# Filler matmuls through the first half of the first chunk's first MoE, in a fused attention and MoE kernel

## Chip, core, metric

One NeuronCore of a Trainium2 chip. The metric is the device time of one execution in microseconds (us), the median of several runs. Before the change it is 1012.5 us (three runs, 1010.94 to 1013.31).

## What is computed

A linear attention with decay over 4 batches, 8 heads, 768 steps and head size 48; its output, as 3072 tokens of 384 numbers, goes through two mixture-of-experts style feed-forward layers (here called the first and the second MoE; each has one expert).

```
for t in range(S):
    cur = einsum('bhd,bhe->bhde', u * k[t], v[t])
    y[t] = einsum('bhd,bhde->bhe', r[t], state + cur)
    state = w[t] * state + einsum('bhd,bhe->bhde', k[t], v[t])
x = y as [B*S, 384]
xn = x / sqrt(mean(x*x) + 1e-6) * rms_g
x = (silu(xn @ w_gate) * (xn @ w_val)) @ w_out        # 384 -> 1536 -> 384
h = relu(x @ w_in)
out = (s * h * h + b) @ moe2_w_out                    # 384 -> 2048 -> 384
```

## The kernel before

The 768 steps are cut into 6 chunks of 128. For each chunk and each of the 4 batches (24 pairs, numbered `jb`) `attention` builds decay products on VectorE (the scans of L340 and L347), scores on TensorE (L379), transposes of k (L383), a small product with u (L388), the masked scores on VectorE (`a`, by L303), the sums `y` (L429, and L422 with the state from chunk 1 on), the new state (L442) and the current step's part (L446). `y` is then normalised on ScalarE and GpSimd, turned by TensorE (L517, in `attention_x`) and split into a high and a low half, `xh` and `xl` (L525), for products in float32r of near float32 accuracy.

A MoE step takes 128 columns of the hidden width (`f`). `mm_in` (L590) makes nine matmuls per product, three pairs of halves times three slices of the 384 inputs; ScalarE and VectorE make the hidden values `sg`, split into `hh` and `hl`; `mm_out` (L575 to L577 in `mm3`) adds three output slices into PSUM banks 2, 3 and 4 over all `f`. The weights come as 64-bit words and are turned into float32 halves, by VectorE for the most part (`weights`, L554 to L566), in the time of the first chunks. The first MoE's first six `f` (`FA`) run over chunk 0 and then chunk 1, then the other six over both; in the first of these four parts the first four `f` go in halves of 256 columns (two batches), the other two over 512.

No engine's order is written out. Every step is given to `Plan.add` with a due time, a cost per engine and the buffers that it reads and writes. `Plan.issue` (L129) is a list scheduler: it walks through time, gives each engine that is free the earliest due step whose inputs are there, and writes the steps out in that order. Each engine's queue runs in that order on the chip, whatever the real times are.

PSUM has 8 banks, `PS`. The attention of chunk 0 takes its banks in turn from a ring (`bank`, L314), six per `jb`: two for scores, one for k's transpose, one for `y`, one for the new state, one for the turned `x`.

A filler is one matmul of zeros, 128x512 in bfloat16, with a weight load of zeros (`idle`, L774). The program begins with 14 of them (`warm`), and the planner adds one wherever it finds PE free with nothing ready, and books `FILL` us for it (L153 to L156). It stops doing so at the first step in `plan.ends`, the first `mm_in`.

Of the kernel before, what the change touches and what calls it, by code (L numbers as in the profile page):

```python
# [22 lines left out]
B, H, S, D = 4, 8, 768, 48  # L23
# [4 lines left out]
KD = DM // 128  # L28
# [20 lines left out]
FA, HALF = 6, (4, 6)  # L49
# [51 lines left out]
class Plan:  # L101
# [6 lines left out]

    PASS = {"pe": 0.20, "pool": 0.10, "act": 0.15, "dve": 0.12, "sp": 2.0}
    SHARED = 6.0  # L110
    FILL = 0.22

    def __init__(self):
        self.idle, self.ends = (None, None), set()
        self.ops, self.deps, self.wrote, self.read = [], [], {}, {}

    def add(self, when, engines, fn, reads=(), writes=(), port=True):
# [82 lines left out]
def mm(n, k=1):  # L200
    return k * (0.013 + n / 2400.0)
# [3 lines left out]
def body(ctx: ExitStack, tc: tile.TileContext, rkw, nat, w1, w2, cst, out):  # L205
    nc = tc.nc
    sb = ctx.enter_context(tc.tile_pool(name="sb", bufs=1))
    ps = ctx.enter_context(tc.tile_pool(name="ps", bufs=1, space=PSUM))
# [67 lines left out]
    plan = Plan()  # L276
# [12 lines left out]
    def op(when, engines, fn, reads=(), writes=(), port=True):  # L289
        if planned[0]:  # L290
            reads, writes = [alias.get(k, k) for k in reads], [alias.get(k, k) for k in writes]
            plan.add(when, engines, fn, reads, writes, port)
        else:
            fn(next(iter(engines)))
# [15 lines left out]
    def ring(name, of):  # L310
        rings[name] = rings.get(name, -1) + 1
        return of[rings[name] % len(of)]

    def bank(jb):  # L314
        return ring("q", (5, 6, 7, 2, 3, 4)) if jb < B else ring("at", (5, 6, 7))

    BOTH = ("dve", "pool")
    DVE, POOL = ("dve",), ("pool",)
# [251 lines left out]
    def slots_of(ph, f):  # L570
        return range(3 * f, 3 * f + 3) if ph == 0 else range(2 * f, 2 * f + 2)
# [7 lines left out]
    def mm_in(t, i, s, x, b0=0, nb=B):  # L579
        n, sl = nb * C, slice(b0 * C, (b0 + nb) * C)  # L580

        dst = PS[i][:, 0:n]

        parts = [[(k, x, b, kk) for b in range(b0, b0 + nb) for kk in range(KD)] for k in ("xh", "xl")]
        passes = ((0, XH), (1, XH)), ((0, XL),)

        def run(e, some, first, last):
            for kk in range(KD):
                for j, (w, xx) in enumerate(some):
                    nc.tensor.matmul(  # L590
                        dst, W[s][:, w, kk * 128:(kk + 1) * 128], xx[x][:, kk, sl], start=first and j == kk == 0,
                        stop=last and kk == KD - 1 and j == len(some) - 1, skip_group_check=True)

        if planned[0] and not plan.ends:
            plan.ends.add(len(plan.ops))
        if t < T0 + 2.0 and planned[0]:
            for p in range(2):
                op(t, {"pe": mm(n, 6 - 3 * p)}, lambda e, p=p: run(e, passes[p], p == 0, p == 1),
                   [("wh", s), ("wl", s)] + parts[p], [("ps", i)])
        else:  # L600
            op(t, {"pe": mm(n, 9)}, lambda e: run(e, ((0, XH), (0, XL), (1, XH)), True, True),
               [("wh", s), ("wl", s)] + parts[0] + parts[1], [("ps", i)])

    def mm_out(t, banks, s, q, first, last, b0=0, nb=B, h0=0):
        n, sl = nb * C, slice(b0 * C, (b0 + nb) * C)
        hs = slice(h0 * C, (h0 + nb) * C)
        for m in range(KD):
            op(t, {"pe": mm(n, 3)}, lambda e, m=m: mm3(
                PS[banks[m]][:, sl], W[s], slice(m * 128, (m + 1) * 128), HH[q][:, hs], HL[q][:, hs],
                first, last), [("wh", s), ("wl", s), ("hh", q), ("hl", q)], [("ps", banks[m])])  # L610

    def store(t, banks, dst, key, b0=0, nb=B):
        n, sl = nb * C, slice(b0 * C, (b0 + nb) * C)
# [132 lines left out]
    def start():  # L746
# [24 lines left out]
                nc.gpsimd.memset(g.rearrange("p h j d -> p (h j d)"), 0.0)  # L771

        def idle():
            nc.tensor.matmul(PS[0], zero[:, 0:128], zero, start=True, stop=True)  # L774

        def warm(e):
            for _ in range(NWARM):
# [5 lines left out]
        op(-199, {"pool": 1.6}, empty, (), [("st", b, p) for b in range(B) for p in range(2)], False)  # L783
        op(-299, {"act": 2.8}, lambda e: nc.scalar.activation(tab, half, AF.Silu), ["c"], ["tab"])
        plan.idle = idle, len(plan.ops)
        op(-300, {"pe": 5.0}, warm, ["z"], [("ps", 0)])

    start()
    steps = []
# [197 lines left out]
```

## Time and profile before

| | us |
|---|---|
| Median of three runs | 1012.5 |
| The profiled execution | 1013.5 |
| Span of its instructions | 1011.6 |
| TensorE busy | 993.0 |
| VectorE busy | 668.9 |
| ScalarE busy | 404.0 |
| GpSimd busy | 215.7 |

PE is TensorE, PEld its weight loads, DVE is VectorE, ACT ScalarE, POOL GpSimd, SP the engine that issues the DMAs. A matmul's row is longer than its share of PE's time, since the next one starts before it ends; what one costs is the distance from its start to the next. The granted clock (PEclk) is a share of 2.4 GHz: 1.00, or 0.50, which is 1.2 GHz. Times in the views are from the span's start.

### The profile page before, as it was taken

To read this page: it belongs to the slowest core of one execution; us is meant where nothing else is said; L and a number is where in the kernel's file an instruction comes from. 1 tells how busy PE (TensorE), PEld (TensorE's weight loads), DVE (VectorE), ACT (ScalarE), POOL (GpSimd) and SP (SyncE) were. 2 spreads that over 40 slices of the span, in tenths; PEclk is the share of its full clock that TensorE was granted. 3 is DMA by queue.
4 is the path that set the end of the run, shared out by engine and by line. 5 is a ranking of instruction groups with operands and counts; after the bars stand their busy time and mean duration, and the time that the engine had idled before them with its cause. 6 is when DMAs were issued, how large, how long until landed. Compare 5 with 4: busy or idle time off the path is not lost.

```text
span 1011.6 us, 14993 instructions
## 1 busy us (share of the span) xinstructions
PE 993.0 (98%) x5873; PEld 834.0 (82%) x5873; DVE 668.9 (66%) x1106; ACT 404.0 (40%) x791; POOL 215.7 (21%) x258
## 2 busy tenths in 40 slices
PE   8989999999999999999999999999999999999997
PEld 5879899888888888888888888887888888888885
DVE  8789997365665565555579889999994443433432
ACT  3334553243554454444434335343343433433333
POOL 4203310114455444445223432000000000000000
PEclk9679999999999999999999999999999999999999
DMA  7343662122221131122276556766660000000001
GB/s 244 111 143 107 212 192 74 40 71 83 83 62 52 51 92 50 52 88 63 68 209 188 177 167 203 250 201 228 235 228 1 1 32 1 32 1 0 32 1 35
DMA packets 44991, 105.19 MB, mean 104 GB/s; under 512 B 3953, under 2 KB 19569, under 8 KB 44913
## 3 DMA queue, kind: packets, MB, share of 16 engines
q1 hardware_dynamic: 44912, 104.16, 32.7%
q8 instruction: 48, 0.79, 0.3%
q14 instruction: 31, 0.25, 0.1%
HBM read 93.14 MB, written 11.01 MB: 103 GB/s over the span
## 4 chain that ended last, share of the span: by engine, by line
PE 95%; DVE 1%; issue 1%; DMA 1%; ACT 1%; POOL 0%; DVEq 0%; ACTq 0%; POOLq 0%
PE b L590 48%; PE b L575 11%; PE b L576 11%; PE b L577 11%; PE b L379 3%; PE b L429 2%; PE b L422 2%; PE b L434 1%; PE b L442 1%; PE b L383 1%; PE b L517 1%; PE b L388 1%; PE b L774 1%; DMA out_t<-o 1%; PE b L446 1%
## 5 line engine op out<-in xcount | busy, mean ns | idle before, releaser
L590 PE MATMUL b<-xh,w 128*128 128x512 f32 (+1 forms) x1566 | 489.4, 377 | 0.5 <-ACT sg L306 0.5
L590 PEld LDWEIGHTS b<-xh,w 128*128 128x128 f32 x1566 | 290.8, 191 | 52.4 <-ACT sg L306 0.7
L590 PE MATMUL b<-xl,w 128*128 128x512 f32 (+1 forms) x783 | 293.0, 375 | 0.0
L575 PE MATMUL b<-hh,w 128*128 128x512 f32 (+1 forms) x537 | 206.6, 385 | 1.8 <-ACT hh L306 1.1
L576 PE MATMUL b<-hl,w 128*128 128x512 f32 (+1 forms) x537 | 203.4, 379 | 2.3 <-DVE hl L303 2.0
L577 PE MATMUL b<-hh,w 128*128 128x512 f32 (+1 forms) x537 | 202.4, 377 | 0.0
L306 ACT ACTIVATE sg<-b 128x512 f32<-128x512 f32 (+1 forms) x179 | 102.1, 571 | 230.9 <-PE b L590 229.4
L590 PEld LDWEIGHTS b<-xl,w 128*128 128x128 f32 x783 | 149.3, 191 | 25.1
L659 DVE SCALAR_TENSOR_TENSOR sg<-sg,cs,b 128x512 f32<-128x512 f32 (+1 forms) x97 | 71.8, 741 | 99.0 <-ACT sg L306 98.9
L576 PEld LDWEIGHTS b<-hl,w 128*128 128x128 f32 x537 | 101.5, 189 | 22.0 <-DVE hl L303 2.4
L575 PEld LDWEIGHTS b<-hh,w 128*128 128x128 f32 x537 | 101.4, 189 | 21.0 <-ACT hh L306 1.7
L577 PEld LDWEIGHTS b<-hh,w 128*128 128x128 f32 x537 | 101.4, 189 | 18.3
L662 DVE SCALAR_TENSOR_TENSOR hl<-sg,cs,hh 128x512 fp32r<-128x512 f32 (+1 forms) x97 | 73.0, 753 | 50.2 <-ACT hh L306 50.2
L306 ACT ACTIVATE hh<-sg,cs 128x512 fp32r<-128x512 f32 (+1 forms) x97 | 69.7, 719 | 84.2 <-DVE sg L659 78.9
L306 ACT ACTIVATE hh<-sg 128x512 fp32r<-128x512 f32 (+1 forms) x82 | 47.5, 579 | 112.7 <-DVE sg L303 112.6
L303 DVE TENSOR_TENSOR sg<-b,sg 128x512 f32<-128x512 f32 (+1 forms) x82 | 51.1, 623 | 51.3 <-PE b L590 49.8
L303 DVE TENSOR_TENSOR hl<-sg,hh 128x512 fp32r<-128x512 f32 (+1 forms) x82 | 53.7, 654 | 13.7 <-ACT hh L306 13.3
L566 POOL TENSOR_TENSOR w<-pat,w 128x384 fp32r<-128x384 f32 x28 | 36.1, 1306 | 65.5 <-ACT w L564 65.5
L401 POOL TENSOR_SCALAR_AFFINE_SELECT a<-a 128x512 f32<-128x512 f32 x38 | 33.1, 890 | 64.7 <-ACT a L306 64.7
L564 ACT ACTIVATE w<-pat 128x384 fp32r<-128x384 f32 x68 | 32.9, 519 | 30.3 <-DVE pat L560 28.7
L560 DVE SCALAR_TENSOR_TENSOR pat<-raw,pat 128x768 uint32<-128x768 uint32 (+1 forms) x40 | 36.1, 908 | 0.0
L558 DVE SCALAR_TENSOR_TENSOR pat<-raw,pat 128x768 uint32<-128x768 uint32 (+1 forms) x40 | 35.8, 899 | 0.1
(122 smaller groups left out, 1011.9 us busy)
## 6 DMA issues: line engine op xcount, KB each, us to landing
raw<-in_w SPq DMA_DIRECT2D x56, 768.0 KB, 4.4
in<-in_rkw SPq DMA_DIRECT2D x24, 448.0 KB, 4.0
raw<-in_w SPq DMA_DIRECT2D x24, 384.0 KB, 3.5
n<-in_nat SPq DMA_DIRECT2D x16, 384.0 KB, 3.1
in<-in_rkw SPq DMA_DIRECT2D x24, 226.6 KB, 2.6
x2d<-o SPq DMA_DIRECT2D x21, 256.0 KB, 2.6
a<-in_rkw SPq DMA_DIRECT2D x24, 224.0 KB, 3.7
v<-in_nat SPq DMA_DIRECT2D x24, 192.0 KB, 3.1
```

The source lines that it names most:

```text
L303: op(when, {e: cost[e] for e in engines}, lambda e: E[e].tensor_tensor(dst, a, b, f), reads, writes, port)
L306: op(when, {"act": act(n)}, lambda e: nc.scalar.activation(dst, src, func, **kw), reads, writes)
L401: op(t, {"pool": 0.60}, lambda e, s=A[p]: nc.gpsimd.affine_select(out=AT[s], in_=AT[s], compare_op=ALU.is_gt, fill=0.0, base=0, pattern=[[ ...
L558: op(t, {"dve": vec2(N)}, lambda e, word=word, pat=pat: nc.vector.scalar_tensor_tensor(pat(), word(1), 0xC0000000, pat(), ALU.bitwise_and, ...
L560: op(t, {"dve": vec2(N)}, lambda e, word=word, pat=pat: nc.vector.scalar_tensor_tensor(pat(), word(0), 29, pat(), ALU.logical_shift_right, ...
L566: op(t, {"dve": vec2(DM)} if ph == 0 else {"dve": vec2(DM), "pool": gps(DM)}, lambda e, c=c, s=s, pat=pat: E[e].tensor_tensor(W[s][:, 1], ...
L575: nc.tensor.matmul(dst, wt[:, 0, cols], xh, start=first, stop=False, skip_group_check=True)
L576: nc.tensor.matmul(dst, wt[:, 0, cols], xl, start=False, stop=False, skip_group_check=True)
L577: nc.tensor.matmul(dst, wt[:, 1, cols], xh, start=False, stop=last, skip_group_check=True)
L590: nc.tensor.matmul(dst, W[s][:, w, kk * 128:(kk + 1) * 128], xx[x][:, kk, sl], start=first and j == kk == 0, stop=last and kk == KD - 1 an ...
L659: op(t, {"dve": vec2(n)}, lambda e: nc.vector.scalar_tensor_tensor(sg, sg, s_col, p, ALU.mult, ALU.mult), [("ps", i)], [("sg", q)], False)
L662: op(t, {"dve": vec2(n)}, lambda e: nc.vector.scalar_tensor_tensor(hl, sg, b_col, hh.bitcast(F32), ALU.add, ALU.subtract), [("sg", q), ("h ...
```

## The change

Four edits. The planner goes on with fillers until the first output step of the sixth `f` of the first part (its weight slot is `slots_of(0, FA - 1)[2]`). It books 0.17 us for each in place of 0.22. The fillers write bank 4, not bank 0: until the first output step has written bank 4 they start afresh (`start=True`), after it they add their zeros to what stands there (`plan.opened`). Bank 4 leaves the ring of chunk 0's attention, which has five banks left.

```diff
--- before.py
+++ after.py
@@ -108,10 +108,10 @@
 
     PASS = {"pe": 0.20, "pool": 0.10, "act": 0.15, "dve": 0.12, "sp": 2.0}
     SHARED = 6.0
-    FILL = 0.22
+    FILL = 0.17
 
     def __init__(self):
-        self.idle, self.ends = (None, None), set()
+        self.idle, self.ends, self.opened = (None, None), set(), False
         self.ops, self.deps, self.wrote, self.read = [], [], {}, {}
 
     def add(self, when, engines, fn, reads=(), writes=(), port=True):
@@ -312,7 +312,7 @@
         return of[rings[name] % len(of)]
 
     def bank(jb):
-        return ring("q", (5, 6, 7, 2, 3, 4)) if jb < B else ring("at", (5, 6, 7))
+        return ring("q", (5, 6, 7, 2, 3)) if jb < B else ring("at", (5, 6, 7))
 
     BOTH = ("dve", "pool")
     DVE, POOL = ("dve",), ("pool",)
@@ -591,8 +591,6 @@
                         dst, W[s][:, w, kk * 128:(kk + 1) * 128], xx[x][:, kk, sl], start=first and j == kk == 0,
                         stop=last and kk == KD - 1 and j == len(some) - 1, skip_group_check=True)
 
-        if planned[0] and not plan.ends:
-            plan.ends.add(len(plan.ops))
         if t < T0 + 2.0 and planned[0]:
             for p in range(2):
                 op(t, {"pe": mm(n, 6 - 3 * p)}, lambda e, p=p: run(e, passes[p], p == 0, p == 1),
@@ -604,10 +602,15 @@
     def mm_out(t, banks, s, q, first, last, b0=0, nb=B, h0=0):
         n, sl = nb * C, slice(b0 * C, (b0 + nb) * C)
         hs = slice(h0 * C, (h0 + nb) * C)
+        if planned[0] and s == slots_of(0, FA - 1)[2]:
+            plan.ends.update(range(len(plan.ops), len(plan.ops) + KD))
+
+        def run(e, m):
+            plan.opened = plan.opened or banks[m] == 4
+            mm3(PS[banks[m]][:, sl], W[s], slice(m * 128, (m + 1) * 128), HH[q][:, hs], HL[q][:, hs], first, last)
+
         for m in range(KD):
-            op(t, {"pe": mm(n, 3)}, lambda e, m=m: mm3(
-                PS[banks[m]][:, sl], W[s], slice(m * 128, (m + 1) * 128), HH[q][:, hs], HL[q][:, hs],
-                first, last), [("wh", s), ("wl", s), ("hh", q), ("hl", q)], [("ps", banks[m])])
+            op(t, {"pe": mm(n, 3)}, lambda e, m=m: run(e, m), [("wh", s), ("wl", s), ("hh", q), ("hl", q)], [("ps", banks[m])])
 
     def store(t, banks, dst, key, b0=0, nb=B):
         n, sl = nb * C, slice(b0 * C, (b0 + nb) * C)
@@ -771,7 +774,7 @@
                 nc.gpsimd.memset(g.rearrange("p h j d -> p (h j d)"), 0.0)
 
         def idle():
-            nc.tensor.matmul(PS[0], zero[:, 0:128], zero, start=True, stop=True)
+            nc.tensor.matmul(PS[4], zero[:, 0:128], zero, start=not plan.opened, stop=True, skip_group_check=True)
 
         def warm(e):
             for _ in range(NWARM):
@@ -783,7 +786,7 @@
         op(-199, {"pool": 1.6}, empty, (), [("st", b, p) for b in range(B) for p in range(2)], False)
         op(-299, {"act": 2.8}, lambda e: nc.scalar.activation(tab, half, AF.Silu), ["c"], ["tab"])
         plan.idle = idle, len(plan.ops)
-        op(-300, {"pe": 5.0}, warm, ["z"], [("ps", 0)])
+        op(-300, {"pe": 5.0}, warm, ["z"], [("ps", 4)])
 
     start()
     steps = []
```

PE's order has 132 fillers after the change and had 47; all its other steps are the same steps. Two products of the state with the decay (L303, 48x192) go from GpSimd's order to VectorE's. The last 4,958 rows of PE's order are the same in both. Two places of it follow. In the names `b_152` to `b_159` are the PSUM banks 0 to 7, `sv_111` the zeros, `in_124` and `in_125` the inputs of the even and the odd `jb`, `xg_135` normalised rows of `y`, `w_75` and up the weight slots.

The first place is PE behind the first batch's attention (`jb` 0), where the second's begins. Before (of the eight L379 rows two stand here):

```order
L446 MATMUL b_154<-av_136,cs_63 128x384
L379 MATMUL b_157<-in_125 128x128
L379 MATMUL b_158<-in_125 128x128
L383 MATMUL b_159<-cs_63,in_125 128x112 x4
L774 LDWEIGHTS sv_111
L774 MATMUL b_152<-sv_111 128x512
L388 MATMUL b_159<-cs_63,l_107 128x2 x4
```

After (one of 22 fillers in a row, and one of two, stand here):

```order
L446 MATMUL b_154<-av_136,cs_63 128x384
L777 LDWEIGHTS sv_111
L777 MATMUL b_156<-sv_111 128x512
L517 MATMUL b_157<-cs_63,xg_135 128x128 x3
L379 MATMUL b_158<-in_125 128x128
L379 MATMUL b_159<-in_125 128x128
L383 MATMUL b_154<-cs_63,in_125 128x112 x4
L388 MATMUL b_154<-cs_63,l_107 128x2 x4
```

The second batch's scores (L379) stood right behind the first batch's last step; now 22 fillers and the turn of the first batch's rows (L517) are between, and its k's transpose goes to bank 2, where the first batch's `y` was.

The second place is PE from the turn of the second batch's rows to the first MoE step's end. After (each row that only repeats is left out):

```order
L517 MATMUL b_158<-cs_63,l_109 128x128 x3
L379 MATMUL b_159<-in_124 128x128
L383 MATMUL b_155<-cs_63,in_124 128x112 x4
L590 MATMUL b_152<-xh_112,w_75 128x256 x6
L388 MATMUL b_155<-cs_63,n_128 128x2 x4
L429 MATMUL b_157<-v_126,a_132 128x48 x4
L442 MATMUL b_158<-v_126,kt_131 64x48
L446 MATMUL b_157<-av_136,cs_63 128x384
L590 MATMUL b_152<-xl_114,w_75 128x256 x3
L590 MATMUL b_153<-xh_112,w_76 128x256
L777 LDWEIGHTS sv_111
L777 MATMUL b_156<-sv_111 128x512
```

Before, five fillers stood behind that L517, then the two products of L590, then the third batch's attention, and no filler came after. Now 19 fillers stand ahead of L517, none from there to the end of the two products, and 15 behind them. Further groups follow: 8 and 6 around the fourth batch's L517, 11 and 15 around the third `f`'s output steps, 2 and 4 in the fifth `jb`.

## Rows read from the trace of the kernel before

**Rows 1.** The page's part 1: busy us, share of the span, instructions

```profile
PE 993.0 (98%) x5873; PEld 834.0 (82%) x5873; DVE 668.9 (66%) x1106; ACT 404.0 (40%) x791; POOL 215.7 (21%) x258
```

**Rows 2.** Waits of PE, 145 to 1012 us: total, times, longest

```profile
PE b L575 <- ACT hh L306: 1.1, 1, 1.1
PE b L575 <- ACT in L623: 0.7, 1, 0.7
PE b L576 <- DVE hl L662: 0.3, 1, 0.3
```

**Rows 3.** The page's part 2: granted clock in 40 slices of 25.3 us

```profile
PEclk9679999999999999999999999999999999999999
```

**Rows 4.** Stretches of 2 us: length, busy by engine, then granted clock, DMA share, GB/s

```profile
32.00:34.00 2.00, 1.58 (x19) 1.49 (x19) 2.00 (x5) 0.78 (x3) 0.00 (x0) 0.60 0.79 229
...
58.00:60.00 2.00, 2.00 (x12) 2.00 (x12) 1.78 (x6) 0.59 (x2) 0.00 (x0) 0.57 0.01 4
...
66.00:68.00 2.00, 2.00 (x14) 2.00 (x13) 2.00 (x4) 0.91 (x2) 0.00 (x0) 0.63 1.02 349
68.00:70.00 2.00, 2.00 (x12) 2.00 (x12) 1.16 (x3) 0.00 (x0) 0.00 (x0) 0.51 0.73 259
```

**Rows 5.** Fillers: weight loads of L774 (ns min/median/max, starts), then PE's timeline, start and us

```profile
L774 PEld LDWEIGHTS <-sv x47: 95/98/181, 1.3 to 26.5; 128*128 128x128 bf16 x47
...
22.09 3.62 PE L774 MATMUL b<-sv 128*128 128x512 bf16 x16
25.54 0.49 PE L517 MATMUL b<-cs,l 128*128 128x128 f32 x3
```

**Rows 6.** PE's timeline, 30 to 66 us; in brackets the idle time ahead and its releaser

```profile
32.42 1.09 PE L442 MATMUL b<-v,kt 128*64 128x48 f32 x16 [0.63 <-ACT kt L306]
...
43.48 1.09 PE L442 MATMUL b<-v,l 128*64 128x48 f32 x16 [0.63 <-ACT l L306]
...
56.36 0.90 PE L517 MATMUL b<-cs,l 128*128 128x128 f32 x3 [2.24 <-ACT l L306]
...
61.58 0.28 PE L576 MATMUL b<-hl,w 128*128 128x256 f32 x1
61.70 0.28 PE L577 MATMUL b<-hh,w 128*128 128x256 f32 x1
...
65.04 0.38 PE L576 MATMUL b<-hl,w 128*128 128x256 f32 x1 [1.97 <-DVE hl L303]
```

**Rows 7.** PE's timeline, 8 to 16 us: the first batch, and the second's scores

```profile
8.56 1.16 PE L379 MATMUL b<-in 48*128 48x128 f32 x16 [1.79 <-DVE in L303]
9.65 0.60 PE L383 MATMUL b<-cs,in 112*128 112x112 f32 x4
...
10.31 0.95 PE L388 MATMUL b<-cs,n 112*128 112x2 f32 x8
...
11.77 1.88 PE L429 MATMUL b<-v,a 128*128 128x48 f32 x16
13.58 0.67 PE L442 MATMUL b<-v,kt 128*64 128x48 f32 x16
14.17 0.91 PE L446 MATMUL b<-av,cs 128*128 128x384 f32 x2
15.01 1.16 PE L379 MATMUL b<-in 48*128 48x128 f32 x16
```

**Rows 8.** Waits of DVE, 34 to 70 us: the three largest

```profile
DVE w L566 <- ACT w L564: 3.2, 1, 3.2
DVE a L303 <- PE b L379: 3.2, 1, 3.2
DVE av L303 <- ACT l L306: 2.2, 1, 2.2
```

**Rows 9.** Waits of PE, 70 to 145 us

```profile
PE b L383 <- DVE xl L525: 0.8, 1, 0.8
PE b L590 <- ACT sg L306: 0.5, 1, 0.5
```

## The prediction, made before the change was run

> **What bounds the kernel now.** I read five views, from coarse to fine. The first, the page's busy line, has TensorE (PE) busy for 993.0 of 1011.6 us and VectorE (DVE), the next, for 668.9 [rows 1]. The reader should see that PE leads, but not yet that it decides, since matmuls overlap. The second is the waits of PE from 145 us to the end: three, 2.1 us in sum [rows 2]. From 145 us on PE simply works through its list, so whatever brings it to that point later or earlier moves the end by as much. The third, the page's 40 slices, says where the first 145 us lose time: PE's granted clock is 6 and 7 tenths in the second and third slice and at the top after that [rows 3]. The fourth, stretches of 2 us, dates it. 0.60 between 32 and 34 us is a full clock (2.4 GHz) until 32.4 us and half (1.2 GHz) from there; 0.57 puts the return at 59.72; 0.63 and 0.51 give a second low stretch from 66.52 to 69.96 [rows 4]. That is 27.32 + 3.44 = 30.76 us at half speed. The fifth, PE's timeline, gives what PE did before the clock fell: after the last filler at 26.5 us [rows 5] came 2.5 us of L590 and then the third batch's attention, many short matmuls and a wait of 0.63 us [rows 6]. The attention of the first two batches, with fillers between its parts, lies before the fall.
>
> The four waits of PE between 30 and 70 us are 0.63 (ACT's copy of kt), 0.63 (the same, next batch), 2.24 (L517 on the normalised rows) and 1.97 us (L576 on `hl`): 5.47 us [rows 6]. The second and third, 2.87 us, lie in the low stretch, so PE worked 30.76 - 2.87 = 27.9 us at half speed. At the full clock that work takes half, so the low clock costs 13.9 us.
>
> **The change, part by part.** PE's time up to 145 us is useful work at the full clock, plus the extra of a low clock, plus waits, plus fillers. The useful work is the same before and after (the order differs in 85 fillers and otherwise in sequence), and the last 4,958 of PE's rows are the same. So the sum needs three terms.
>
> *Fillers.* 132 in place of 47. One costs the distance from start to start: 16 of them from 22.09 to 25.54 us, 0.2156 us each [rows 5]. 85 x 0.2156 = 18.3 us added. Their weight loads lie beside them (98 ns each). They wait for nothing after the first, because the zeros are ready at the start and bank 4 is written by PE alone until the part's end. Now some of them accumulate where all before overwrote; no row of before shows that for these matmuls, but L576 and L577, which both accumulate into one bank, start 0.12 us apart, about what 256 columns need [rows 6], so I take no surcharge.
>
> *The planner's 0.17.* It books 0.17 us for what takes 0.2156. A planned gap thus gets more fillers than fit it, and PE comes 0.046 us later per filler to the step behind. That is inside the 18.3 us. It has a good side: a group outlasts the wait that it covers. The wait for L517 was 3.45 us in the second batch (22.09 to 25.54 us, [rows 5]); the new groups in front of L517 have 22, 19, 15 and 8+ fillers, that is 4.7, 4.1, 3.2 and 1.7 us.
>
> *Five banks in place of six.* The second batch's scores now stand behind the first batch's L517 and 22 fillers: in place of 15.01 us [rows 7] they start at about 15.0 + 22 x 0.2156 + 0.3 = 20.1 us, 5 us later. Since the time is filled with fillers it is not counted again. What is late next is VectorE: its mask and the `xl` of each batch move back, so the third batch's mask comes some 2 us later than now. The bounds of a new PE wait from this: nothing, if the fillers overrun it; 3.2 us, the largest wait of VectorE on this chain now, at the top [rows 8]. Two state products move from GpSimd to VectorE, beside PE.
>
> *What the clock gives back.* If the clock holds at 2.4 GHz through the first part, 13.9 us, and with the fillers in place of waits up to 5.47 us more: 19.4 us.
>
> Sum: 19.4 - 18.3 = 1.1 us gained, less new waits between 0 and 3.2 us. I take 0.5, near the lower end, because I followed the new order by hand with the full-clock durations of [rows 7] and found L517, the masks and the split weights ready before PE got through its fillers nearly every time. That leaves **-0.6 us**. It is a wash: the fillers take the time that the clock returns. The profiled execution took 1013.5 us, its span 1011.6; the three timed runs have a median of 1012.5, so the profiled one is 1.0 above. By its own time the change gives 1012.9; against the median 1012.5 - 0.6 = **1011.9 us**. A measurement of this kernel tells about 0.2%, 2.0 us, from no change.
>
> **Rivals.**
>
> *The clock falls all the same, in the third batch* (slower). In the new order PE runs from the second batch's L517 to the next 15 fillers without one: scores, transposes, six L590, L388, L429, L442, L446 and the rest of the first two L590 groups. From the rows of the first batch that is 1.1 + 0.6 + 0.7 + 0.9 + 1.8 + 0.6 + 0.8 + 1.4 = 7.9 us (18 L590 at 0.12; L383 and L388 by their own durations, the others from start to start) [rows 6, 7]. Before, the clock fell 5.9 us after the last filler, with much the same work [rows 4, 5]. For it: the same mix and no filler. Against it: no wait stands in the stretch now, and the first batch's 11.8 to 15.0 us, with no filler either, kept the full clock. It decides if the granted clock drops between about 33 and 40 us. The price of one low stretch is half of 3.44 us; two of them, 3.4 us: 1015.3 us. Chance 0.15. The Trainium skill bears on this (TensorE: Matmul & The Clock Gate, "A second HAM failure mode: psum-queue depth-cycling"): a kernel that cycles through PSUM banks makes PE pause briefly between groups so often that its clock swings between two levels. The trace agrees that a fall needs no long wait; by that rule five banks in place of six speak against this change, and the time would be this rival's.
>
> *The waits after 70 us go too* (faster). Two waits remain in before, 0.8 us at L383 and 0.5 us at L590 [rows 9]. If VectorE is ahead there by then, and no new wait comes, 19.4 + 1.3 - 18.3 = 2.4 us: 1010.1 us. VectorE's three largest waits between 34 and 70 us, 3.2, 3.2 and 2.2, are the room for it [rows 8]. Chance 0.15.
>
> *The weights come late* (slower). The chain of five banks puts the first four batches in series, and VectorE, which splits the weights too, then leaves PE waiting behind the fillers. The point from which it decides is a delay of VectorE that outlasts the groups; with the upper bound of 3.2 us and no 0.5, 1011.9 + 2.7 = 1014.6 us. Chance 0.07.
>
> *PE is not the bound* (much faster). If the fillers lay in time that PE has to spare, the 18.3 us would cost nothing and the whole 19.4 us stay: 993.1 us. Against it: 2.1 us of waits in 866 us [rows 2]. Chance 0.02. The Trainium skill (Perfetto Trace Analysis, "Identifying the Most-Contended Engine") says that matmul busy time is a poor measure of what TensorE has left and the busy share of the weight loads a better one. That share is 82% here [rows 1], which by the rule leaves room; I go by the waits, which leave none.
>
> *The change does not do what it says.* Fillers of zeros might not hold the clock among attention steps; then the low stretches stay, the fillers come on top, and with the waits they replace it is 1012.5 + 18.3 - 5.5 = 1025.3 us. Against it: before, with fillers, the clock was full until 32.4 us. Chance 0.03.
>
> **How the numbers follow.** The forecast, a clock that holds and a small remainder, has 0.58. Its own range is 1010.8 (no new wait, and part of the waits after 70 us) to 1014.4 (near the upper bound of the waits): all within 0.2% but for its edges. Faster by over 0.2%: 0.15 + 0.02 = 0.17. Slower: 0.15 + 0.07 + 0.03 = 0.25. Same: 0.58. The range takes in the faster rival at 1010.1 and the slower at 1015.3 and leaves out 993 and 1025, 1 in 20, and the tails of the rest: 1009.9 to 1015.4.
>
> **What the profile after would show.** Right: granted clock at the top from the first slice to the last but the start; 132 fillers of about 28 us in sum counted start to start; PE waits between 10 and 145 us under 2 us; VectorE's three largest waits between 34 and 70 us under 5 us in sum. The first rival: a stretch of 2 us with a clock of 0.5 to 0.8 between 33 and 45 us. The weights' rival: new PE waits on `w` or `hl` behind a group of fillers. I am wrong in the main if PE's fillers and useful work after 70 us no longer add up to the span, or if PE shows waits after 145 us that are not there now.

## The result and the profile after

The changed kernel is **slower by 0.7%**: 1016.78 us, the median of 18 runs (1012.62 to 1022.27), against 1010.66 for the kernel before, run beside it on the same chips (18 runs, 1003.57 to 1019.24). The ratio is 1.0071, with a 95% interval of 1.0050 to 1.0093. The forecast was 1011.9, at most 1015.4. The profiled execution took 1018.22 us. Runs over 1.5% above the fastest of the same kernel count as slow and are left out of the ratios and of what is fitted below: one of these 18 (1019.24), and 13 of the 130 of the kernel before that were made beside the experiments (1021 to 1026 us, at mean clocks of 0.973 to 0.979).

The page of the kernel after: its span, the busy line, the granted clock, and the fillers' group.

```profile
span 1016.5 us, 15168 instructions
...
PE 1005.5 (99%) x5958; PEld 834.7 (82%) x5958; DVE 667.1 (66%) x1108; ACT 403.9 (40%) x791; POOL 210.3 (21%) x256
...
PEclk7999999999999999999999999999999999999999
...
L777 PE MATMUL b<-sv 128*128 128x512 bf16 x132 | 35.7, 421 | 1.3 <-DVE col L759 1.3
```

Read it against [rows 1, 3]. PE is busier by 12.5 us; GpSimd is less busy by 5.4 us, and the other engines do what they did. The two low slices in the time of the MoE, 6 and 7 tenths in [rows 3], are full now. A low one has appeared where none was, in the first slice. The stretches of 2 us date it (same columns as [rows 4]):

```profile
8.00:10.00 2.00, 0.90 (x12) 0.90 (x14) 2.00 (x3) 0.00 (x0) 0.00 (x0) 0.91 1.06 381
10.00:12.00 2.00, 2.00 (x14) 1.46 (x11) 2.00 (x5) 0.00 (x0) 0.59 (x2) 0.50 0.99 363
...
22.00:24.00 2.00, 2.00 (x8) 0.75 (x6) 0.06 (x1) 0.53 (x2) 1.64 (x5) 0.68 0.88 295
24.00:26.00 2.00, 2.00 (x11) 0.88 (x9) 0.00 (x0) 0.59 (x2) 0.00 (x0) 1.00 0.19 77
...
66.00:68.00 2.00, 2.00 (x13) 1.13 (x13) 2.00 (x5) 0.20 (x1) 0.00 (x0) 1.00 0.66 201
68.00:70.00 2.00, 2.00 (x15) 1.58 (x14) 2.00 (x5) 0.00 (x0) 0.00 (x0) 1.00 0.33 97
```

0.91 of a full clock between 8 and 10 us is a fall to half (1.2 GHz) at 9.64; 0.68 is the return (2.4 GHz) at 23.28. From there on every stretch is at 1.00, those around 66 to 70 us too, which were low before [rows 4]. The low time is 13.6 us, not 30.8, and lies under the first batch's attention instead of the third's. What PE did before the fall: it ran its first fillers, waited 1.77 us for VectorE's `in`, and began the first scores.

PE's waits from 0 to 145 us, all of 0.2 us and more, then (after the "...") from 145 us to the end:

```profile
PE b L379 <- DVE in L303: 1.8, 1, 1.8
PE b L777 <- DVE col L759: 1.3, 1, 1.3
...
PE b L575 <- ACT in L626: 0.7, 1, 0.7
PE b L575 <- DVE o L628: 0.2, 1, 0.2
```

Both of the first two stood there before too (the 1.79 in [rows 7] is one). The four waits of [rows 6] and the two of [rows 9] are gone, 6.8 us, and 1.2 of the 2.1 us after 145 us [rows 2].

PE's timeline where the second batch begins:

```profile
20.98 6.06 PE L777 MATMUL b<-sv 128*128 128x512 bf16 x22
26.88 0.49 PE L517 MATMUL b<-cs,xg 128*128 128x128 f32 x3
27.30 1.16 PE L379 MATMUL b<-in 48*128 48x128 f32 x16
```

The second batch's scores start at 27.30 us; before it was 15.01 [rows 7], and the prediction said 20.1. The low clock made the first batch 6 us late, and the fillers are the other 6.

The sum of these two executions, each row of PE taken from its start to the next one's, less idle time: fillers take 32.8 us in place of 12.1 (85 x 0.2156 is 18.3; most of the rest is that 11 of them ran at the half clock), useful rows 972.6 in place of 980.9, and PE idles 4.5 us in place of 11.9. That is +20.7 - 8.2 - 7.4 = +5.1 us to PE's last row; the spans differ by 4.9.

The useful rows ran 9.3 us at the half clock in place of 27.9, and gave back 8.2, less than half of the difference: in these traces a row does not take quite twice as long at the half clock. Two rows of the kernel before, in its second low stretch, start 0.21 us apart; the same two lines at the full clock start 0.12 apart [rows 6]:

```profile
67.24 0.41 PE L576 MATMUL b<-hl,w 128*128 128x256 f32 x1
67.45 0.41 PE L577 MATMUL b<-hh,w 128*128 128x256 f32 x1
```

### The profile page after: what moved, and what is told of

It reads as the page before. It is cut to its first block, busy times and chain, and to the rows that moved or that the text cites. A ratio compares the mean times of both kernels' runs of the same rounds, so it can differ in the third digit from the quotient of the medians.

```text
span 1016.5 us, 15168 instructions
## 1 busy us (share of the span) xinstructions
PE 1005.5 (99%) x5958; PEld 834.7 (82%) x5958; DVE 667.1 (66%) x1108; ACT 403.9 (40%) x791; POOL 210.3 (21%) x256
## 4 chain that ended last, share of the span: by engine, by line
PE 91%; DVE 4%; DMA 3%; issue 1%; ACT 1%; POOL 0%; SPq 0%; ACTq 0%; DVEq 0%
PE b L590 45%; PE b L575 10%; PE b L576 10%; PE b L577 10%; PE b L379 3%; PE b L777 2%; PE b L429 2%; PE b L422 2%; PE b L434 1%; PE b L442 1%; PE b L383 1%; PE b L517 1%; DVE ws L720 1%; PE b L388 1%; DMA xl<-x2d 1%
## 5 line engine op out<-in xcount | busy, mean ns | idle before, releaser
L590 PE MATMUL b<-xh,w 128*128 128x512 f32 (+1 forms) x1566 | 486.8, 375 | 0.1
L590 PEld LDWEIGHTS b<-xh,w 128*128 128x128 f32 x1566 | 287.6, 188 | 52.6 <-DVE sg L303 0.3
L590 PE MATMUL b<-xl,w 128*128 128x512 f32 (+1 forms) x783 | 291.5, 373 | 0.0
L576 PE MATMUL b<-hl,w 128*128 128x512 f32 (+1 forms) x537 | 202.9, 378 | 0.4
L590 PEld LDWEIGHTS b<-xl,w 128*128 128x128 f32 x783 | 147.4, 188 | 25.6
L576 PEld LDWEIGHTS b<-hl,w 128*128 128x128 f32 x537 | 101.1, 188 | 20.5 <-DVE hl L665 2.5
L577 PEld LDWEIGHTS b<-hh,w 128*128 128x128 f32 x537 | 101.0, 188 | 18.3
L303 DVE TENSOR_TENSOR sg<-b,sg 128x512 f32<-128x512 f32 (+1 forms) x82 | 51.1, 624 | 58.0 <-PE b L590 54.8
L303 DVE TENSOR_TENSOR hl<-sg,hh 128x512 fp32r<-128x512 f32 (+1 forms) x82 | 53.6, 654 | 15.2 <-ACT hh L306 15.0
L566 POOL TENSOR_TENSOR w<-pat,w 128x384 fp32r<-128x384 f32 x28 | 33.7, 1219 | 68.2 <-ACT w L564 68.2
L401 POOL TENSOR_SCALAR_AFFINE_SELECT a<-a 128x512 f32<-128x512 f32 x38 | 28.9, 781 | 71.5 <-ACT a L306 71.5
L525 DVE SCALAR_TENSOR_TENSOR xl<-b,cs,xh 128x128 fp32r<-128x128 f32 x72 | 20.8, 345 | 28.8 <-ACT xh L306 28.7
L777 PE MATMUL b<-sv 128*128 128x512 bf16 x132 | 35.7, 421 | 1.3 <-DVE col L759 1.3
```

Source lines behind the costliest of these rows:

```text
L303: op(when, {e: cost[e] for e in engines}, lambda e: E[e].tensor_tensor(dst, a, b, f), reads, writes, port)
L566: op(t, {"dve": vec2(DM)} if ph == 0 else {"dve": vec2(DM), "pool": gps(DM)}, lambda e, c=c, s=s, pat=pat: E[e].tensor_tensor(W[s][:, 1], ...
L576: nc.tensor.matmul(dst, wt[:, 0, cols], xl, start=False, stop=False, skip_group_check=True)
L577: nc.tensor.matmul(dst, wt[:, 1, cols], xh, start=False, stop=last, skip_group_check=True)
L590: nc.tensor.matmul(dst, W[s][:, w, kk * 128:(kk + 1) * 128], xx[x][:, kk, sl], start=first and j == kk == 0, stop=last and kk == KD - 1 an ...
L777: nc.tensor.matmul(PS[4], zero[:, 0:128], zero, start=not plan.opened, stop=True, skip_group_check=True)
```

## Experiments

My first theory was that the change is mostly a trade of fillers against the clock, in which the fillers cost more than they return. The rivals put the loss on one of the three other edits: five banks in place of six, the planner's 0.17, or where the fillers lie. Every run also carries its mean granted clock, which turned out to be the most useful number: for most kernels here the time follows it nearly in a straight line (not for e9_pow, whose clock hardly moved, and e14_half). Below, "at clock 1" is where a least-squares line through the runs of that kernel ends. For the kernel before, through 117 runs made beside the experiments, it is 1003.1 us with 0.68 us more per 0.001 of clock lost (mean clock 0.9888, median 1011.1 us, mean 1010.7). For the changed kernel it is 1011.7 us, with 0.89 per 0.001 (mean clock 0.9939, mean 1017.1 us). The standard error of such an end is 0.4 us for the kernel before, 0.8 for the changed one and 1 to 3 for most of the sets of 11 or 12 runs, so differences of 1 or 2 us between these ends say little. A ratio is to the kernel before, run beside the same set (its medians were 1010.4 to 1012.8).

**e1_banks.** Five banks alone, on the kernel before; its fillers still stop at the first `mm_in` (62 of them).

```diff
-        return ring("q", (5, 6, 7, 2, 3, 4)) if jb < B else ring("at", (5, 6, 7))
+        return ring("q", (5, 6, 7, 2, 3)) if jb < B else ring("at", (5, 6, 7))
...
-            nc.tensor.matmul(PS[0], zero[:, 0:128], zero, start=True, stop=True)
+            nc.tensor.matmul(PS[4], zero[:, 0:128], zero, start=True, stop=True)
```

> Five banks alone: the kernel before with chunk 0's attention in five banks, the fillers in bank 4, still ending at the first L590, 0.22 us booked. PE's order has 62 fillers (47 before, 132 after). Theory A (PE's own list decides: time is useful work, plus fillers, plus low clock, plus PE's waits): 15 fillers at 0.2156 us are 3.2 us, and the clock may fall in the first MoE as it did before: 2 to 4 us over the kernel before, with a granted clock near 0.985. Theory B (the series of the first four batches, made by the five banks, is the cost, by late VectorE work): all or most of the 6 us that the change costs, 5 to 7 us over before, with PE waits on hl, w or xh that were not there. Theory C (only the stretch at the start, where the clock was low in the profile after, is to blame, and that by chance): within 2 us of before.

Measured: 1017.46 us (1013.14 to 1023.93), ratio 1.0062 [1.0041, 1.0084]. With 15 of the 85 fillers, nearly the whole loss is there. Its profiled execution (1022.0 us span, at a clock of 0.980 the lowest of its 11 runs) shows a part of why. PE's timeline:

```profile
14.91 4.05 PE L774 MATMUL b<-sv 128*128 128x512 bf16 x18
21.49 0.55 PE L517 MATMUL b<-cs,xg 128*128 128x128 f32 x3 [2.52 <-ACT xg L306]
21.96 1.40 PE L379 MATMUL b<-in 48*128 48x128 f32 x16
```

and GpSimd's:

```profile
14.82 5.36 POOL L303 TENSOR_TENSOR st<-st,pm 64x192 f32<-64x192 f32 x2 [4.53 <-ACT st L306]
20.26 0.56 POOL L466 TENSOR_TENSOR rs<-rs,col 128x1 f32<-128x1 f32 x1
```

With five banks the second batch's scores are behind the first batch's L517. L517 waits for ScalarE's normalised rows, these for GpSimd's `rs` (a power, L466), and that stands on GpSimd's queue behind two products of the state. These took 5.36 us, the power came at 20.26, and PE, 18 fillers later, stood idle for 2.52 us. The same two rows of the kernel before:

```profile
14.82 2.95 POOL L303 TENSOR_TENSOR st<-st,pm 64x192 f32<-64x192 f32 x2 [4.53 <-ACT st L306]
17.85 0.56 POOL L466 TENSOR_TENSOR rs<-rs,col 128x1 f32<-128x1 f32 x1
```

GpSimd's order is the same there, but PE was at the second batch's scores from 15.01 us [rows 7] and nobody waited. After the idle time the clock fell, in e1_banks (it fell three more times between 50 and 78 us, and once at 548):

```profile
20.00:22.00 2.00, 0.51 (x5) 0.35 (x5) 0.00 (x0) 1.15 (x3) 0.96 (x4) 1.00 0.58 243
22.00:24.00 2.00, 2.00 (x21) 1.78 (x21) 0.93 (x4) 1.44 (x5) 0.00 (x0) 0.68 0.00 0
24.00:26.00 2.00, 2.00 (x11) 1.88 (x10) 1.13 (x2) 0.00 (x0) 0.00 (x0) 0.50 0.34 68
```

**e2_fill22.** The change with the planner's old price of a filler (112 fillers).

```diff
-    FILL = 0.17
+    FILL = 0.22
```

> The changed kernel with 0.22 us booked for a filler in place of 0.17: 112 fillers in place of 132, all else as planned anew. Theory A: 20 fillers less are 4.3 us less than the changed kernel, 1 to 3 us over the kernel before, clock above 0.99. Theory B: the banks are as in the changed kernel, so the time is too, 5 to 7 us over before. Theory C: as the changed kernel within 2 us.

Measured: 1017.13 us (1013.27 to 1019.68), 1.0048 [1.0026, 1.0069]. Not clearly better with 20 fillers fewer, 4.3 us by the count: at clock 1 it is 1010.5, 1.2 under the change. Its trace has the same 2.5 us wait at the first L517, and its clock fell too, at 20.8 us, within that wait.

**e4_fill17.** The kernel before with 0.17 (54 fillers).

```diff
-    FILL = 0.22
+    FILL = 0.17
```

> The kernel before with 0.17 us booked for a filler in place of 0.22, six banks, fillers ending at the first L590: 54 fillers in place of 47. Theory A: 7 fillers are 1.5 us; 0 to 3 us over the kernel before, clock as before. Theories B and C: as the kernel before within 2 us.

Measured: 1013.37 us (1009.91 to 1017.61), 1.0024 [1.0002, 1.0046]. Seven fillers are 1.5 us, and the loss (2.4 us by the ratio, with 0.2 to 4.6 in its interval) can't be told from that: no sign that the price does more by itself.

**e3_mute.** The order of the change, without its 61 fillers behind the first `mm_in` (71 left).

```diff
+            mute = mute or i == self.first
             if i < 0:
-                idle()
+                if not mute:
+                    idle()
...
+        if planned[0] and plan.first is None:
+            plan.first = len(plan.ops)
```

> The changed kernel's order on every engine, with the 61 fillers behind the first L590 left out of it (71 of 132 stay). Nothing else moves. Theory A: 61 fillers are 13.2 us; PE's waits for L517 and for weights come back in their place (3 to 8 us) and the clock may fall again in the first MoE (up to 5 us): 1 to 8 us less than the changed kernel, and PE waits of 3 us and more ahead of L517. Theory B: the order is unchanged, so the late VectorE work is too, and the time is that of the changed kernel within 2 us. If the fillers are a pure cost, 13 us less than the changed kernel, 7 under the kernel before.

Measured: 1017.2 us (1012.56 to 1020.49), 1.0063 [1.0038, 1.0088]; mean clock 0.9874. So the new fillers in the MoE cost nothing in sum: 61 of them, 13.2 us, are gone and the time is the same. In the two traces, from row to row, the fillers take 13.0 us less, PE idles 6.8 us more and the useful rows take 6.4 us more, at a clock lower by 0.0065 on the mean. What sets this order apart from the kernel before is then five banks and 24 more fillers at the start, and it is as slow as the whole change.

**e7_mutelate.** The same order; here only the 46 fillers behind the first output step into bank 4 are left out (86 left).

```diff
             if i < 0:
-                idle()
+                if not self.opened:
+                    idle()
```

> The changed kernel's order with the 46 fillers behind the first output step into bank 4 left out (86 of 132 stay). Theory D: those stand where PE waits for VectorE anyway, so the time is the changed kernel's within 2 us, with PE waits on hl and w in their place. Theory A: 46 fillers are 9.9 us, less waits of 4: 5 us under the changed kernel. The clock should stay at the changed kernel's 0.994 if the groups ahead of the fourth batch's turn hold it, and fall to 0.988 to 0.990 if the late ones do.

Measured: 1012.27 us (1009.12 to 1020.41), 1.0017 [0.9983, 1.0050]; the kernel before stood at 1012.8 in these runs. The 15 fillers between the first `mm_in` and that output step bring the mean clock from 0.9874 to 0.9927, nearly free. The 46 later ones, those that add zeros into the open accumulator, bring 0.0012 more, about 1 us, and cost some 5 at clock 1 (1006.7 to 1011.7).

**e6_six.** Six banks kept: fillers into bank 0 up to the first `mm_in`, none while bank 4 is in the ring, then into bank 4 to the sixth `f` (94 fillers).

```diff
+        if planned[0] and plan.again is None:
+            plan.again = len(plan.ops) + KD - 1
...
-            nc.tensor.matmul(PS[0], zero[:, 0:128], zero, start=True, stop=True)
+            nc.tensor.matmul(PS[4 if plan.opened else 0], zero[:, 0:128], zero, start=not plan.opened, stop=True, skip_group_check=True)
```

> The change with six banks: chunk 0's attention keeps bank 4 in its ring; the fillers write bank 0 up to the first L590, none are set from there to the first output step into bank 4, and from then to the sixth f's output step they add zeros into bank 4; 0.17 us booked. 94 fillers (47 before, 132 after). Theory D (the five banks, which put the first four batches in series, are what the change costs; fillers only take the place of waits and pay for the clock): within 2 us of the kernel before, well under the changed kernel. Theory A (fillers cost their own length): 47 more fillers are 10.1 us, less waits of 3 and clock of 4: 2 to 5 us over before. Granted clock as in the kernel before, 0.988, if the clock falls in the third batch's attention, ahead of these fillers; over 0.99 if they bring it back sooner.

Measured: 1015.22 us (1011.52 to 1019.54), 1.0032 [1.0002, 1.0062]; mean clock 0.9888, that of the kernel before. The late fillers without the early ones do not hold the clock, which in its trace is low from 34 to 55 us, ahead of them. All the change's fillers with six banks were not run.

**e5_spot, e10_spot4, e15_spot4.** One kernel, run in three sets: the kernel before plus 16 fillers written by hand, four behind k's transposes (L383) and four behind the u product (L388) of the third and the fourth batch, into bank 4 ahead of its next use.

```diff
+    def spot():
+        zero = SV.rearrange("p a h d -> p (a h d)")[:, 0:NB]
+        for _ in range(4):
+            nc.tensor.matmul(PS[4], zero[:, 0:128], zero, start=True, stop=True, skip_group_check=True)
...
+            if jb in (2, 3):
+                spot()
```

> The kernel before with 16 fillers more, in groups of four into bank 4 behind the transposes (L383) and behind L388 of the third and of the fourth batch; six banks, no replanning. 16 x 0.2156 = 3.4 us, less the waits of 0.63 us that two of the groups cover: 2.2 us net. If four fillers in each place hold the clock in these two attentions, the mean granted clock is 0.996 in place of 0.988 and gives back 0.8 us per 0.001, 6 us: 3 to 5 us under the kernel before. If they don't, 2 us over it with a clock of 0.986 to 0.99.

> The kernel before with 16 spot fillers, once more and with more rounds, to tell whether it beats the kernel before: 4 to 6 us under it, clock 0.995 in most runs. The change's own aim (a held clock) reached with 16 fillers and six banks; if it is not under before by at least 2 us here, the first run's 1006.5 was chance.

> The kernel before with 16 spot fillers, a third time: median 1004 to 1007, ratio 0.993 to 0.998, most runs at a clock of 0.995 and more and a few at 0.985 (6 us and more longer).

Measured: 1006.53 us, 0.9958 [0.9919, 0.9997]; then 1005.65, 0.9981 [0.9941, 1.0021]; then 1007.02, 0.9995 [0.9957, 1.0032]. The median of all 35 runs is 1006.6, some 4.5 us under the kernel before; their mean is 1008.3, 2.3 under its mean. 28 of them lie at a clock of 0.994 or more (1003.5 to 1008.3 us) and seven at 0.984 to 0.985 (1016.4 to 1019.3), and these few keep the intervals wide: only the first excludes no change. So a gain in time is likely and not shown beyond doubt. Sixteen fillers in the place where the clock was lost raised the mean clock to 0.993 to 0.995, as far as the change's 85 did. The page of e10_spot4:

```profile
span 1001.5 us, 15022 instructions
...
PEclk9999999999999999999999999999999999999999
```

Its waits of PE from 8 to 145 us (its lines are 5 to 9 higher by the added ones):

```profile
PE b L526 <- ACT l L306: 2.4, 1, 2.4
PE b L585 <- DVE hl L303: 2.2, 2, 2.0
PE b L384 <- DVE in L303: 1.4, 1, 1.4
```

At a nearly full clock (0.997) the long waits stay: L526 and L585 are before's L517 and L576. A held clock does not remove them; in the change, with fillers in their place, they are gone.

**e11_spot2.** The same with two fillers per group (8 in all).

```diff
-        for _ in range(4):
+        for _ in range(2):
```

> The same with groups of two, 8 fillers more than before, 1.7 us less fillers than with groups of four. If two in a place hold the clock as four do, 1 to 2 us under the run with four, at a clock of 0.995; if they hold it less often, runs of 0.985 to 0.988 come back and the median is between that and the kernel before.

Measured: 1006.88 us (1004.42 to 1016.6), 0.9981 [0.9948, 1.0013]. Not to be told from four.

**e8_warm.** The kernel before with 22 fillers at the start, not 14, to close PE's first wait, for the case that this wait is what the later fall goes back to.

```diff
-NWARM = 14
+NWARM = 22
```

> The kernel before with 22 fillers at the start in place of 14. The first 16 end at 6.8 us and the first scores start at 8.6, held by VectorE, so 8 more fit in the wait (1.7 us) and cost nothing. If the clock that is low in some runs falls because of that wait (as in the profile after, 9.8 to 23.4 us), the runs of 0.985 to 0.988 become fewer and the median falls by 1 to 3 us; if not, within 1 us of the kernel before.

Measured: 1012.57 us (1005.61 to 1015.99), 1.0014 [0.9983, 1.0045]; mean clock 0.9885, against 0.9888 without. With six banks the first wait does not decide it. Its profiled execution held the clock (0.997), and behind the start it has the order of the kernel before, row by row. The 139 rows of PE that ran at the half clock there and at the full one here took 25.8 us there and 14.6 here: 1.76 times as long, not twice.

**e9_pow.** The change, with the state products of the first chunk made to read `rs`, so that GpSimd does the power first.

```diff
-                    tt(t + LATE, BOTH, HP * D, s, s, pmb, ALU.mult, [("pm", q)], [("st", b, p)])
+                    tt(t + LATE, BOTH, HP * D, s, s, pmb, ALU.mult, [("pm", q), ("rs", q)], [("st", b, p)])
```

> The changed kernel, with the first four batches' state products made to wait for GpSimd's power of the row norm (L466), so that GpSimd takes the power first. In the profiles with five banks the power stands behind two state products on GpSimd (5.4 us in the run with the late fillers left out, 3.0 us before), the turn of the first batch (L517) waits for it, and with five banks the second batch's scores stand behind that turn: PE idles 1.7 to 2.5 us behind its fillers at 19 to 21 us, and the clock falls at 21 to 23 us in four profiles of five. 142 fillers are planned, 18 in place of 22 ahead of the first L517. Theory D1 (that wait and the fall behind it are what five banks cost): no PE wait at the first L517, second scores near 19 us, clock at 0.997, 3 to 5 us under the changed kernel. Theory D2 (the series itself costs, whatever GpSimd does): within 2 us of the changed kernel, clock 0.994.

Measured: 1015.15 us (1014.62 to 1018.21), 1.0054 [1.0031, 1.0077]; the planner puts in 142 fillers here. The clock was 0.997 to 0.999 in each of its 11 runs. GpSimd:

```profile
16.37 2.48 POOL L466 TENSOR_TENSOR rs<-rs,col 128x1 f32<-128x1 f32 x1 [6.03 <-ACT rs L306]
18.82 1.08 POOL L303 TENSOR_TENSOR st<-st,pm 64x192 f32<-64x192 f32 x2
```

PE:

```profile
15.40 3.83 PE L777 MATMUL b<-sv 128*128 128x512 bf16 x17
19.51 0.55 PE L517 MATMUL b<-cs,xg 128*128 128x128 f32 x3 [0.28 <-ACT xg L306]
19.99 1.16 PE L379 MATMUL b<-in 48*128 48x128 f32 x16
```

The scores start at 19.99 us, the prediction's 20.1, and the wait at L517 is 0.28 in place of 2.52. This is the case on which the forecast rested, and it is still slower than before. 20 of the 117 runs of the kernel before had a clock of 0.995 or more, and their median is 1005.4: at a held clock this form costs 9.8 us. Its 95 more fillers are 20.5 us by the count. Against e8_warm, whose trace also has a held clock, its trace has 17.4 us more of fillers and 6.0 us less of idle time on PE. So half of the fillers' length or more came on top and did not replace a wait.

**e12_both.** e7_mutelate and e9_pow together (87 fillers).

> Both at once: the changed kernel with GpSimd's power first, as in the run of that alone, and without the fillers behind the first output step into bank 4 (87 stay). Theory D1: 3 to 5 us under the run without the late fillers (1012.3), 1007 to 1009, under the kernel before, clock 0.996. Theory D2: 1011 to 1013.

Measured: 1014.29 us (1011.4 to 1018.0), 1.0044 [1.0015, 1.0074], mean clock 0.9920. No gain over e7_mutelate: in its trace the clock held to 60 us and fell then, where the fillers left out would have stood. The expectation was 1007 to 1009 us if the power's place was the fault; so to put the power first does not help in this order.

**e13_bankpow.** e1_banks with the power first (59 fillers).

> Five banks alone (0.22 us booked, fillers ending at the first L590) with GpSimd's power of the row norm ahead of the state products: 59 fillers, 12 more than before, 2.6 us. If five banks cost only by the wait at the first L517 and the fall of the clock behind it: 4 us under five banks alone (1017.5), 1012 to 1014, and at the same granted clock 1 to 3 us over the kernel before. If the series of the four batches costs by itself: 1016 to 1018 as five banks alone.

Measured: 1012.09 us (1007.21 to 1018.11), 1.0010 [0.9981, 1.0039], 5.4 us under e1_banks. So five banks alone cost little by putting the batches in series and much by what that exposed: the power behind the state products, PE's wait for it, and the clock (mean 0.9876, and 0.9904 with the power first). Its own trace can't show the wait gone: the clock fell at 10.9 us there, PE came to the first L517 late and waited for nothing, and a later L517 waited 2.5 us. The trace of e9_pow shows it (0.28 us).

**e14_half.** The change with each of its 132 fillers half as wide.

```diff
-            nc.tensor.matmul(PS[4], zero[:, 0:128], zero, start=not plan.opened, stop=True, skip_group_check=True)
+            nc.tensor.matmul(PS[4][:, 0:256], zero[:, 0:128], zero[:, 0:256], start=not plan.opened, stop=True, skip_group_check=True)
```

> The changed kernel with each of its 132 fillers 256 columns wide in place of 512, nothing else; the 14 at the start are halved too. PE's order and every wait's place are the changed kernel's. 116 fillers behind the start, 0.108 us less each, are 12.5 us less. Theory A (their length is the cost): PE waits come back for a part of it, and 3 to 6 us under the changed kernel at the same clock remain; the clock may fall more often (down to 0.988, up to 4 us back). If the five banks' series is the cost, the time is the changed kernel's within 2 us, with waits in the fillers' place, at the same clock.

Measured: 1011.86 us (1009.71 to 1016.79), 1.0018 [0.9986, 1.0051]. About 5 us come back from half of the fillers' length, at a mean clock of 0.9909, below the change's 0.9939.

## Why the prediction was wrong

It gave -0.6 us, and +6.1 was measured by the medians (+6.4 by the means that the sum below uses). Step by step:

*PE decides the end from 145 us on*: right. 0.9 us of waits there after the change, and the fillers' length shows in the time (e2_fill22, e9_pow, e14_half).

*Fillers*, 18.3 us, no surcharge for adding into an open accumulator: not contradicted. The 22 in PE's timeline span 20.98 to 26.88 us, of which 2.3 lay at the low clock; the other 3.6 hold some 17 at 0.2156. The 46 that accumulate start 0.216 us apart within their groups as well; they cost some 5 us at clock 1 for 9.9 us of their length, so some of it still replaced waits. The sum left out that fillers, too, are longer at a low clock: 11 in the trace after, over 2 us.

*The waits that they replace*: right in kind. The prediction had 5.47 us in its sum and 1.3 in a rival; all are gone in the trace after, and no new wait came in it.

*What the clock gives back*, 13.9 us: **the step that failed.** Some 2 to 5 us came back on the mean, and three things in the step were wrong. The work at the half clock was taken to need half the time at the full one; the rows of e8_warm say 1/1.76, which makes the 27.9 us worth 12. The price was read from one execution with a lower clock than most: 0.983, and only 19 of the 130 runs of the kernel before are as low. Over the 117 runs the mean is 0.9888, and 0.0112 at 0.68 us per 0.001 is 7.6 us. And the clock was taken to hold: the changed kernel's mean is 0.9939, and 0.0061 at 0.89 is 5.4 us still lost. So 7.6 - 5.4 = 2.2 us come back. (Fitted through all 130 runs, the kernel before has 1001.8 us at clock 1 and 0.81 per 0.001; it then loses 10.1 us, and 4.7 come back.) In the two profiled executions, where the kernel before had the low clock, it is 8.2 us of useful rows, of which the slower fillers take over 2.

*Five banks in place of six*: doubtful too, in the half us that it left for new waits. It took the 3.45 us of L517 in the second batch as the wait that 22 fillers had to cover in the first, and forgot that two state products precede the power on GpSimd there. From the end of L446 to L517 it was 6.4 us in e1_banks (15.07 to 21.49), against 4.7 of fillers. In e1_banks, e2_fill22, e3_mute and e7_mutelate, PE ran dry there by 1.7 to 2.5 us and the clock fell between 20 and 23 us; with the power first, e13_bankpow was 5.4 us faster than e1_banks. In the profiled execution of the change itself the clock fell earlier, at 9.64 us, and the late PE then waited for nothing. Which of the two falls the other runs of the change had is not seen, as only one left a trace. How much of the loss is the banks' in the changed kernel stays open: with the power first, e9_pow was only 1.6 us under the change, with 10 fillers more, and e12_both not under e7_mutelate.

*The new sum*, by the two lines: at clock 1 the kernels are 1011.7 - 1003.1 = 8.6 us apart, which is 18.3 us of fillers less 9.7 that they replaced, whatever the banks added included. The clock returns 2.2. That is +6.4, the distance of the two means. A least-squares line goes through its mean, so this sum has to close; it shows how the loss divides and is no second measurement. With all 130 runs the parts are 8.4 replaced and 4.7 returned. Set against the prediction's terms, the fillers replaced more than the 5.5 us of waits that it had, and the clock returned some 9 to 12 us less.

*Its own signs.* Two of those for being right came out: no PE wait between 10 and 145 us, and a full clock but for the start. Two did not: the fillers take 32.8 us, not 28, and VectorE's largest waits from 34 to 70 us come to 5.7 us, not under 5. None of them tested the price of the clock.

*The rivals.* The clock did not fall in the third batch: from 24 us on every stretch is at 1.00. It fell in another place, the first batch's scores, behind a wait of 1.77 us that stood there before too, and not in a stretch of short matmuls without filler and without waits. That this rival's time (1015.3) was nearest to the measured is luck in the main. Late weights: no wait on `w` or `hl` in the trace after. PE not the bound: excluded by e14_half and e9_pow. That zeros do not hold the clock: excluded by e3_mute against e7_mutelate.

## What to carry to other kernels

Before a clock loss is priced from a profile, compare that execution's mean clock with those of the other runs, and price the typical one; here the prize read from one profile (13.9 us) was well above what the mean run loses (8 to 10). Take the price from rows that stand in the profile at both levels, not from the ratio of the clocks. Put few fillers where the clock falls (8 or 16 did as much for the mean clock as 85), and let each fill time in which PE would wait, since in e9_pow, where the clock held, half of the fillers' length or more was lost. A buffer taken from a ring changes what a queue's order means: look through every engine on the new chain for work that stands ahead of the step that has become urgent.

## What the runs showed of the hardware

The granted clock differs from run to run of one program: means of 0.978 to 0.997 for the kernel before, in 26 runs on one chip. A fall came without long idle time: PE's waits ahead of it were 0.63 us [rows 6], 1.77 us and 1.7 to 2.5 us. Nor did such a wait always bring one: 1.79 us at the same place in the kernel before were followed by a full clock up to 32.4 us [rows 4, 7]. With the fillers of e9_pow no run of 11 lost it.

GpSimd's small operations took very unequal times (its spans are rough): the same two state products 1.08, 2.95 and 5.36 us, the power on 128 numbers 0.56 or 2.48. Beside the 5.36 us of e1_banks VectorE's timeline has

```profile
15.40 1.42 DVE L558 SCALAR_TENSOR_TENSOR pat<-raw,pat 128x768 uint32<-128x768 uint32 x2
16.74 1.42 DVE L560 SCALAR_TENSOR_TENSOR pat<-raw,pat 128x768 uint32<-128x768 uint32 x2
18.08 1.22 DVE L340 TENSOR_TENSOR_SCAN eb<-in,ones 112x516 f32<-112x516 f32 x1
```

and beside the 2.95 us of the kernel before

```profile
15.41 1.42 DVE L558 SCALAR_TENSOR_TENSOR pat<-raw,pat 128x768 uint32<-128x768 uint32 x2
16.74 0.69 DVE L303 TENSOR_TENSOR a<-b,mk 128x512 f32<-128x512 f32 x1
17.34 0.69 DVE L303 TENSOR_TENSOR l<-b,mk 128x512 f32<-128x512 f32 x1
```

In the first, VectorE reads two SBUF operands until 19.3 us and GpSimd ends at 20.2; in the second L558 ends at 16.8, the masks, with one of their operands in a PSUM bank, come at 16.74 and GpSimd ends at 17.8. In the trace after, L340 ends at 22.06 and the two products at 22.94. So in all three they end some 0.9 us after VectorE's last row with two SBUF operands. In e9_pow the products took 1.08 us from 18.82, when VectorE had paused. The Trainium skill (GPSIMD Engine Reference, "Specifications") says that GpSimd shares its SBUF interfaces with VectorE, with contention where a VectorE instruction has two SBUF inputs. The traces agree with that; no run here tried it by itself. If it is the cause, the changed order of VectorE, too, lengthened the chain to the first L517.
